# Weight preparation shared out anew over 64 expert steps, and the first weight chunks and token products moved

## The chip, the cores and the metric

The kernel runs on one NeuronCore of a Trainium2 chip. The metric is device time in microseconds (us), lower is better; several executions are timed and their median counts. One execution is also recorded by the hardware profiler, and its rows are what is read here.

The core has five engines with a queue of instructions each: TensorE (PE) multiplies matrices, VectorE (DVE), ScalarE (ACT) and GpSimd (POOL) compute element by element, SyncE (SP) issues most DMA transfers. They meet through semaphores; on its own queue each engine works strictly in order.

## The reference

Three blocks in a chain, cut to what matters:

```python
# 1. gated linear attention, B=4, H=8, S=768, D=48
f = 1 / (1 + exp(-f_logit))
state = f[t] * state + outer(k[t], v[t]);  y[t] = q[t] @ state
x = y as 3072 tokens x 384
# 2. mixture of 8 experts, the best one for each token
e = argmax(normalized(x) @ normalized(expert_emb).T / tau)
x = gate[:, None] * (relu(x @ w1[e]) @ w2[e])       # 384 -> 1024 -> 384
# 3. gated block
out = ((x @ w_a) * (x @ w_b)) @ w_out               # 384 -> 1536 -> 384
```

Inputs and outputs are float32 (w_a, w_b and w_out come as 64-bit floats of two words, which the kernel turns into 32 bits itself). Matrix products are made of a high and a low part of each operand, three products for each exact one.

## The kernel before

**Stages.** The attention scan lies from 0 to about 145 us, the experts from about 147 to 372 us, the gated block from there to the end at 805 us. The change touches the experts' stage and the first visits of the gated block.

**Expert steps.** The loop over s = 0 to 63 handles expert e = s // 8 and, with j = s % 8, one eighth of its hidden layer. A step issues, in this order: `h_part(s)`, nine matmuls into the PSUM tile `ph` (L1213 to L1215), ACT's high part `hh` (L1236) and DVE's low part `hl` (L1237) of its result; for j = 3 to 5 `x_turn`, a turn of the next expert's token rows, which gives DVE a subtraction (L1207); then `prep_run`, the weight preparation; then `w_more`, the splitting of the next experts' weights; and last `y_part(s - 1)`, nine matmuls into `po` (L1256), of which the last three read `hl` of the step before. The tile sizes tell the expert: 448 columns is expert 1 (steps 8 to 15), 432 expert 2, 416 expert 3, down to 384 for expert 7 (steps 56 to 63). After an expert's last product its outputs are copied to `yT` (L1272 on DVE).

So what `prep_run` and `w_more` give DVE in step s stands on DVE's queue behind `hl` of step s and ahead of `hl` of step s + 1.

**Weight preparation.** `prep_run(s, us)` gets a budget of planned microseconds: 1.4 in the first expert's steps, 2.1 in all others. It first runs what is due (deferred splits and stores), then takes pieces from two generators, `combines` first and `conv` with what remains, until the budget is used up; each piece states a planned cost. A piece that begins with budget left is finished, so a step can go over.

- `conv` turns weights to 32 bits, 18 blocks of 128x1536 words: ACT's absolute value, then DVE's L950 and L951 (planned 1.15), then L954 (0.95), then L957 for w_out or L988 for w_a and w_b (0.95). The blocks of w_out are split one slot later into high part (ACT) and low part (POOL, L964) and stored to DRAM. Three of the w_out blocks come first, those of w_a and w_b behind them; of the last three some pieces run in the gated block's slots.
- `combines` forms 15 weight matrices each of w_a (`combine(0)`) and of w_b (`combine(1)`) by sums on DVE (L1000, L1001, planned 0.7 each). A step later each is split by ACT and by POOL, in a few cases by DVE (L1036), and a step after that SP stores it to the DRAM tensor `wst` (L1056). Only when `combine(1)` is through, and s is over 60, are chunks 0 to 2 loaded by `w_chunk`.

**Splitting expert weights.** `w_more` runs `job_run`: every other step ACT makes the high part of a 128x1536 block, POOL subtracts two thirds of it and DVE one third (L895), so POOL is busy with a pair of subtractions in odd steps.

**Gated block.** A chunk of `wst` has eight matrices of 128x256 for each 128 partitions; `w_chunk(h)` loads one into a ring of three places (8 rows for even h, 7 for odd). They lie in the tile that held the last experts' weights, so a load waits for those products. `visit` multiplies six token products with six weight products (L1468 into `pv` and `pw`); every eight slots form a round of k1, k4, c1, k2, k5, c2, k3, k6, of which k4, k5 and k6 belong to the round before and are not made in round 0. Results go to `acc` by ACT (L1471 to L1475) and DVE (L1478, L1484). `prep_run` goes on every third slot with a budget of 1.0, and `x_prep` makes the token products: sums (L1348), ACT's high part (L1365) and the low part (L1356, DVE). The first group of them, `x_first`, is made on DVE during the last eight steps and the first three slots. `gate_ops` are the gate's small operations on DVE and ACT. Later on output products (L1497 to L1501 into `pq`) run between the visits.

**What sets the order.** It is written out by hand: instructions go to each engine's queue in the order in which the Python code issues them, and the budgets decide in which step a piece is issued. Before the change the lines in question are (the calls):

Of the kernel before, what the change touches and what calls it, by code (L numbers as in the profile page):

```python
# [6 lines left out]
F32 = mybir.dt.float32  # L7
# [21 lines left out]
NTT = NT // XT  # L29
# [18 lines left out]
NU = 8  # L48
# [8 lines left out]
def build(tc, I, out, dbg=None):  # L57
# [92 lines left out]
    with tc.manual_schedule():  # L150
# [920 lines left out]
                yield None  # L1071

        def w_chunk(h):
            if h < 2 * (NTT * NU + 1):
                n = 8 if h % 2 == 0 else 7
                SP.dma_start(out=WR[h % 3][:, 0:n].bitcast(F32), in_=wst[h % (2 * NU), :, 0:n])

        def combines():
            while phase[0] < 1:
                yield None  # L1080
            yield from combine(0)
            phase[0] = max(phase[0], 2)
            free[3] = free[4] = now[0]
            while phase[0] < 3:
                yield None
            free[3] = free[4] = free[5] = 1e9
            yield from combine(1)
            free[4] = now[0]
            phase[0] = 4
            while now[0] <= NE * FJ - 4:  # L1090
                yield None
            for h in range(3):
                w_chunk(h)

        streams = [combines(), conv()]

# [224 lines left out]
        def x_more():  # L1321
            for t in [t for t in acts if t not in X[NE - 1]] + list(X[NE - 1]):
                XS.extend(flat(t)[:, i * 512:(i + 1) * 512] for i in range(3))
# [48 lines left out]
        for s in range(NE * FJ):  # L1372
            e, j = divmod(s, FJ)
            h_part(s)
            if s == 0:
                ids_copy(0)
                rows_load_n(2)
                ids_store(0)
            if j == 0:
                y_part(s - 1)  # L1380
            if 3 <= j <= 5:
                x_turn(e + 1, j - 3)
            prep_run(s, 1.4 if s < FJ else 2.1)
            w_more(s)
            if 1 <= s <= 3:
                next(count_ops)
            n = 4 if e == 0 else 3
            if 0 <= j - 3 < n and e + 1 < NE:
                row_sq(e + 1, CAPS[e + 1] // 4, *[i for i in range(4) if min(i, n - 1) == j - 3])
            if j == n + 2:  # L1390
                ids_copy(e + 1)
            if j == n + 3 and e + 1 < NE:
                ids_store(e + 1)
                if e > 0:
                    rows_load_n(e + 2)
            if j > 0:
                y_part(s - 1)
            if s == IDS:
                SP.dma_start(out=idf, in_=heads[0:NT].rearrange("(t p) w -> p t w", p=128))
            if s == IDS + 4:  # L1400
                pf = ps_t.tile([128, 4, HP], F32, tag="t", name="pt")[:, 0, 0:1]
                T.matmul(out=pf, lhsT=ones[0:1], rhs=flag_b, start=True, stop=True)
                V.tensor_copy(fl_sb, pf)
                V.scalar_tensor_tensor(out=idx, in0=fl_sb.to_broadcast([128, NT // 128]), scalar=float(NT), in1=idf[:, :, 0],
                                       op0=ALU.mult, op1=ALU.add)
            if s == IDS:
                x_more()
            if s == IDS - 1:
                next(x_first)
            if s >= IDS:  # L1410
                for _ in range((2, 2, 1, 1, 1, 1, 3)[s - IDS]):
                    next(x_first, None)
            if s == IDS + 5:
                next(gate_ops)
# [127 lines left out]
        for at in range(8 * (NTT * NU + 1)):  # L1542
            P, rho = divmod(at, 8)
            if rho % 4 == 0 and at:
                w_chunk(at // 4 + 2)
            if at < 3:
                for _ in range(2):
                    next(x_first, None)
            name, late = SLOTS[rho]
# [247 lines left out]
```

## Time and profile before

| | |
|---|---|
| median of 3 runs | 808.38 us (807.41 to 810.64) |
| the profiled execution, its own time | 807.06 us |
| its span, first to last instruction | 805.2 us |
| mean granted TensorE clock | 0.990 |
| TensorE busy | 765.9 us (95%) |
| VectorE busy | 604.2 us (75%) |
| ScalarE busy | 419.8 us (52%) |
| GpSimd busy | 413.5 us (51%) |

Times in rows count from the span's start. A bracket at the end of a timeline row is the time for which the engine stood idle before it, and whose instruction ended that. Matmuls are pipelined, so rows of TensorE overlap. The granted clock is a share of full speed: 1.00 is 2.4 GHz, 0.50 is 1.2 GHz.

### The profile page before, as it was taken

To read this page: it belongs to the slowest core of one execution; us is meant where nothing else is said; L and a number is where in the kernel's file an instruction comes from. 1 tells how busy PE (TensorE), PEld (TensorE's weight loads), DVE (VectorE), ACT (ScalarE), POOL (GpSimd) and SP (SyncE) were. 2 spreads that over 40 slices of the span, in tenths; PEclk is the share of its full clock that TensorE was granted. 3 is DMA by queue.
4 is the path that set the end of the run, shared out by engine and by line. 5 is a ranking of instruction groups with operands and counts; after the bars stand their busy time and mean duration, and the time that the engine had idled before them with its cause. 6 is when DMAs were issued, how large, how long until landed. Compare 5 with 4: busy or idle time off the path is not lost.

```text
span 805.2 us, 16800 instructions
## 1 busy us (share of the span) xinstructions
PE 765.9 (95%) x6354; PEld 736.4 (91%) x6354; DVE 604.2 (75%) x1007; ACT 419.8 (52%) x889; POOL 413.5 (51%) x392
## 2 busy tenths in 40 slices
PE   7899989999999989988899999999999999999995
PEld 5899988989999989977798999999999999999995
DVE  7999995699978877696989567756766765686552
ACT  5899973666565746653444334434434434444331
POOL 6667773363468936972354154445326525343314
PEclk9999999999999999999999999999999999999998
DMA  7989752888499985978997998889888888988982
GB/s 278 327 301 325 238 189 88 277 275 266 154 294 265 325 270 150 289 215 290 345 414 266 352 323 302 301 299 339 309 297 328 312 294 320 330 297 295 335 305 88
DMA packets 83087, 226.82 MB, mean 282 GB/s; under 512 B 10649, under 2 KB 42247, under 8 KB 76727
## 3 DMA queue, kind: packets, MB, share of 16 engines
q1 hardware_dynamic: 79639, 216.10, 79.1%
q0 software_dynamic: 3072, 9.56, 3.1%
q8 instruction: 52, 0.85, 0.4%
q14 instruction: 36, 0.29, 0.1%
q10 hardware_dynamic: 288, 0.02, 0.0%
HBM read 192.95 MB, written 32.70 MB: 280 GB/s over the span
## 4 chain that ended last, share of the span: by engine, by line
PE 60%; DVE 19%; DMA 8%; issue 5%; ACT 4%; POOL 2%; SPq 0%; DVEq 0%; POOLq 0%; ACTq 0%
PE pv L1468 19%; PE po L1256 7%; PE pw L1468 5%; PE pq L1501 4%; PE pq L1499 4%; PE pq L1497 4%; DMA w<-wst 4%; PE ph L1213 3%; PE ph L1215 3%; PE ph L1214 3%; DVE a L1356 2%; DVE Rt L241 2%; DVE big L1445 2%; DVE big L1484 2%; DMA qkf<-qkf 2%
## 5 line engine op out<-in xcount | busy, mean ns | idle before, releaser
L1450 POOL TENSOR_TENSOR w<-big,w 128x512 fp32r<-128x512 f32 x72 | 94.7, 1330 | 172.6 <-ACT w L1449 169.8
L1468 PE MATMUL pv<-w,w 128*128 128x256 f32 x912 | 135.5, 283 | 9.1 <-DMA w<-wst 4.4
L1484 DVE TENSOR_TENSOR big<-big,pv 128x512 f32<-128x512 f32 x144 | 98.3, 682 | 58.3 <-PE pv L1468 58.3
L1468 PEld LDWEIGHTS pv<-w,w 128*128 128x128 f32 x912 | 126.3, 189 | 13.6 <-DVE big L1484 4.0
L1468 PE MATMUL pv<-a,w 128*128 128x256 f32 x816 | 120.3, 281 | 0.3
L1468 PEld LDWEIGHTS pv<-a,w 128*128 128x128 f32 x816 | 113.5, 188 | 2.1 <-DVE big L1478 1.1
L895 POOL TENSOR_TENSOR w<-raw,w 128x512 fp32r<-128x512 f32 x48 | 79.2, 1671 | 44.4 <-ACT w L892 41.1
L1501 PE MATMUL pq<-raw,w 128*128 128x384 f32 x288 | 97.2, 338 | 1.0 <-POOL w L1450 1.0
L1497 PE MATMUL pq<-raw,w 128*128 128x384 f32 x288 | 97.3, 338 | 0.0
L1499 PE MATMUL pq<-raw,w 128*128 128x384 f32 x288 | 96.9, 337 | 0.0
L1256 PE MATMUL po<-hh,w 128*128 128x224 f32 (+7 forms) x384 | 80.4, 344 | 0.0
L1478 DVE TENSOR_TENSOR big<-big,pv 128x256 f32<-128x256 f32 x96 | 40.3, 420 | 49.7 <-PE pv L1468 47.9
L1256 PEld LDWEIGHTS po<-hh,w 128*128 128x128 f32 x384 | 66.8, 190 | 1.3 <-DVE yT L1272 0.2
L1213 PE MATMUL ph<-a,w 128*128 128x224 f32 (+7 forms) x192 | 66.4, 346 | 0.0
L1215 PE MATMUL ph<-a,w 128*128 128x224 f32 (+7 forms) x192 | 66.3, 345 | 0.0
L1214 PE MATMUL ph<-a,w 128*128 128x224 f32 (+7 forms) x192 | 66.2, 345 | 0.0
L1445 DVE TENSOR_TENSOR big<-big 128x512 f32<-128x512 f32 x72 | 64.9, 929 | 1.7
L1449 ACT ACTIVATE w<-big 128x512 fp32r<-128x512 f32 x72 | 44.8, 633 | 37.0 <-DVE big L1445 37.0
L1236 ACT ACTIVATE hh<-ph 128x224 fp32r<-128x224 f32 (+7 forms) x64 | 31.4, 490 | 60.0 <-PE ph L1215 57.2
L1475 ACT ACTIVATE big<-pw 128x256 f32<-128x256 f32 x48 | 18.3, 382 | 78.1 <-PE pw L1468 78.1
L1501 PEld LDWEIGHTS pq<-raw,w 128*128 128x128 f32 x288 | 54.3, 189 | 1.6 <-POOL w L1450 1.6
L1256 PE MATMUL po<-hl,w 128*128 128x224 f32 (+7 forms) x192 | 45.6, 346 | 9.7 <-DVE hl L1237 9.6
(275 smaller groups left out, 1745.8 us busy)
## 6 DMA issues: line engine op xcount, KB each, us to landing
w<-wst SPq DMA_DIRECT2D x49, 1024.0 KB
w<-wst SPq DMA_DIRECT2D x49, 896.0 KB
raw<-wost SPq DMA_DIRECT2D x72, 384.0 KB
raw<-moe_w SPq DMA_DIRECT2D x32, 768.0 KB
qkf<-qkf SPq DMA_DIRECT2D x20, 768.0 KB
wst<-big SPq DMA_DIRECT2D x21, 512.0 KB
vx<-vx SPq DMA_DIRECT2D x24, 192.0 KB
big<-moe_w_out SPq DMA_DIRECT2D x6, 768.0 KB
```

The lines of the kernel that those rows point to most:

```text
L895: (G if i < NPOOL else V).tensor_tensor(out=wt[:, 1, f], in0=raw[:, f], in1=wt[:, 0, f].bitcast(F32), op=ALU.subtract)
L1213: T.matmul(out=out, lhsT=wh, rhs=xh, start=first, stop=False)
L1214: T.matmul(out=out, lhsT=wl, rhs=xh, start=False, stop=False)
L1215: T.matmul(out=out, lhsT=wh, rhs=xl, start=False, stop=last)
L1256: T.matmul(out=OS[e][k], lhsT=w[:, j % 4, k * 128:(k + 1) * 128], rhs=x, start=(j == 0 and w is wh and x is hh), stop=(j == FJ - 1 and x i ...
L1445: V.tensor_tensor(out=a, in0=a, in1=b, op=ALU.mult)
L1450: G.tensor_tensor(out=g[:, 1], in0=a, in1=g[:, 0].bitcast(F32), op=ALU.subtract)
L1468: T.matmul(out=out, lhsT=wt, rhs=xt_, start=first and j == 0, stop=j == 2, skip_group_check=True)
L1484: V.tensor_tensor(out=o, in0=o, in1=bank, op=ALU.subtract)
L1497: T.matmul(out=q, lhsT=gh, rhs=wh, start=(f == 0), stop=False)
L1499: T.matmul(out=q, lhsT=gh, rhs=wl, start=False, stop=False)
L1501: T.matmul(out=q, lhsT=gl, rhs=wh, start=False, stop=(f == F2J - 1))
```

## The change

Three things are changed.

- The budget of `prep_run` from step 8 on becomes 1.7 in steps with j = 3 to 5, those with a turn of rows, and 2.6 in the others, in place of 2.1 in all. Over eight steps that is 18.1 planned microseconds in place of 16.8.
- Chunk 0 is loaded at the end of step 60, chunk 1 at the end of step 62, both without the rows that round 0 does not read; only chunk 2 still waits for `combine(1)`.
- Of the token products, none is made in steps 61 and 62; the two moved pieces follow behind slot 3, which had none.

```diff
--- before.py
+++ after.py
@@ -1071,7 +1071,10 @@
                 yield None
 
         def w_chunk(h):
-            if h < 2 * (NTT * NU + 1):
+            if h < 2:
+                for lo, hi in ((0, 2), (4, 8)) if h == 0 else ((2, 5),):
+                    SP.dma_start(out=WR[h][:, lo:hi].bitcast(F32), in_=wst[h, :, lo:hi])
+            elif h < 2 * (NTT * NU + 1):
                 n = 8 if h % 2 == 0 else 7
                 SP.dma_start(out=WR[h % 3][:, 0:n].bitcast(F32), in_=wst[h % (2 * NU), :, 0:n])
 
@@ -1089,8 +1092,7 @@
             phase[0] = 4
             while now[0] <= NE * FJ - 4:
                 yield None
-            for h in range(3):
-                w_chunk(h)
+            w_chunk(2)
 
         streams = [combines(), conv()]
 
@@ -1380,7 +1382,7 @@
                 y_part(s - 1)
             if 3 <= j <= 5:
                 x_turn(e + 1, j - 3)
-            prep_run(s, 1.4 if s < FJ else 2.1)
+            prep_run(s, 1.4 if s < FJ else 1.7 if 3 <= j <= 5 else 2.6)
             w_more(s)
             if 1 <= s <= 3:
                 next(count_ops)
@@ -1405,10 +1407,12 @@
                                        op0=ALU.mult, op1=ALU.add)
             if s == IDS:
                 x_more()
+            if s in (NE * FJ - 4, NE * FJ - 2):
+                w_chunk((s + 4 - NE * FJ) // 2)
             if s == IDS - 1:
                 next(x_first)
             if s >= IDS:
-                for _ in range((2, 2, 1, 1, 1, 1, 3)[s - IDS]):
+                for _ in range((2, 2, 1, 1, 0, 0, 3)[s - IDS]):
                     next(x_first, None)
             if s == IDS + 5:
                 next(gate_ops)
@@ -1543,7 +1547,7 @@
             P, rho = divmod(at, 8)
             if rho % 4 == 0 and at:
                 w_chunk(at // 4 + 2)
-            if at < 3:
+            if at < 4:
                 for _ in range(2):
                     next(x_first, None)
             name, late = SLOTS[rho]
```

After the change all lines below the first piece of the diff have moved: L1207, L1237, L1272 and L1440 of before are L1209, L1239, L1274 and L1444.

**Place 1, DVE in steps 16 and 17.** Ahead of the first `hl` shown, that of step 17, there stand the pieces of step 16; between the first and the second `hl` those of step 17. L950 to L988 are one block of `conv`, L895 is DVE's third of a weight split. Before:

```order
L950 TENSOR_SCALAR ct<-ct 128x768
L951 TENSOR_SCALAR ct<-ct 128x768
L1237 SCALAR_TENSOR_TENSOR hl<-ph,hh 128x432
L954 SCALAR_TENSOR_TENSOR big<-big,ct 128x768
L988 SCALAR_TENSOR_TENSOR yT_2532<-big 128x256
L988 SCALAR_TENSOR_TENSOR yT_2533<-big 128x256
L988 SCALAR_TENSOR_TENSOR yT_2534<-big 128x256
L895 TENSOR_TENSOR w_2524<-raw,w_2524 128x512
L1237 SCALAR_TENSOR_TENSOR hl<-ph,hh 128x432
```

After:

```order
L950 TENSOR_SCALAR ct<-ct 128x768
L951 TENSOR_SCALAR ct<-ct 128x768
L954 SCALAR_TENSOR_TENSOR big<-big,ct 128x768
L988 SCALAR_TENSOR_TENSOR yT_2532<-big 128x256
L988 SCALAR_TENSOR_TENSOR yT_2533<-big 128x256
L988 SCALAR_TENSOR_TENSOR yT_2534<-big 128x256
L1239 SCALAR_TENSOR_TENSOR hl<-ph,hh 128x432
L895 TENSOR_TENSOR w_2524<-raw,w_2524 128x512
L1239 SCALAR_TENSOR_TENSOR hl<-ph,hh 128x432
```

L954 and three L988 have moved from behind `hl` of step 17 to ahead of it.

In the same way L957 of step 9, alone, has moved from behind `hl` of step 9 to ahead of it.

**Place 2, DVE in steps 24 to 26.** The three `hl` are those of steps 25, 26 and 27; L1000 is a sum of `combine(0)`, L1036 a low part of such a sum. Before:

```order
L1237 SCALAR_TENSOR_TENSOR hl<-ph,hh 128x416
L950 TENSOR_SCALAR ct<-ct 128x768
L951 TENSOR_SCALAR ct<-ct 128x768
L1036 TENSOR_TENSOR big<-yT_2533,big 128x4x128
L895 TENSOR_TENSOR w_66<-raw,w_66 128x512
L1237 SCALAR_TENSOR_TENSOR hl<-ph,hh 128x416
L1000 TENSOR_TENSOR yT_2534<-yT_2534,yT_2532 128x512
L1000 TENSOR_TENSOR yT_2533<-yT_2532,yT_2534 128x512
L954 SCALAR_TENSOR_TENSOR big<-big,ct 128x768
L1237 SCALAR_TENSOR_TENSOR hl<-ph,hh 128x416
```

After:

```order
L950 TENSOR_SCALAR ct<-ct 128x768
L951 TENSOR_SCALAR ct<-ct 128x768
L954 SCALAR_TENSOR_TENSOR big<-big,ct 128x768
L1036 TENSOR_TENSOR big<-yT_2533,big 128x4x128
L1239 SCALAR_TENSOR_TENSOR hl<-ph,hh 128x416
L1000 TENSOR_TENSOR yT_2534<-yT_2534,yT_2532 128x512
L1000 TENSOR_TENSOR yT_2533<-yT_2532,yT_2534 128x512
L988 SCALAR_TENSOR_TENSOR big<-big 128x3x256
L895 TENSOR_TENSOR w_66<-raw,w_66 128x512
L1239 SCALAR_TENSOR_TENSOR hl<-ph,hh 128x416 x2
```

L954 has moved ahead of `hl` of step 25, and the two L1000 ahead of `hl` of step 26, with an L988 that came later before; nothing is left between the last two `hl`.

**Place 3, SP at the end of the expert steps.** L1056 stores a product of `combine(1)`, L1076 (L1079 is the other branch after the change) loads a chunk, L1440 and L925 load a w_out block and a part of w_out. Before:

```order
L1056 DMA wst<-big 128x3x256
L1056 DMA wst<-big 128x256
L1056 DMA wst<-big 128x3x256
L1056 DMA wst<-big 128x256
L1056 DMA wst<-big 128x4x256
L1076 DMA w_2524<-wst 128x2048
L1076 DMA w_2524<-wst 128x1792
L1076 DMA w_2524<-wst 128x2048
L1440 DMA raw<-wost 128x768 x2
L925 DMA big<-moe_w_out 128x2x768
```

After:

```order
L1056 DMA wst<-big 128x3x256
L1056 DMA wst<-big 128x256
L1056 DMA wst<-big 128x3x256
L1056 DMA wst<-big 128x256
L1076 DMA w_2524<-wst 128x512
L1076 DMA w_2524<-wst 128x1024
L1056 DMA wst<-big 128x4x256
L1079 DMA w_2524<-wst 128x2048
L1076 DMA w_2524<-wst 128x768
L925 DMA big<-moe_w_out 128x2x768
L1444 DMA raw<-wost 128x768 x2
```

Chunk 0, now of two pieces, stands ahead of the last store; chunk 2 stands ahead of chunk 1.

Elsewhere on DVE, ACT and POOL the new budgets move pieces by one or two steps in the same manner. Steps 34 and 35 hold what steps 35 and 36 held (the two L1000 and L950, L951), steps 29 to 31 hold more than before, `combine(1)` comes to its end in step 59 in place of 60, and the three last blocks of `conv` in the gated block come three slots earlier. The POOL splits that follow from a sum or a block move with it.

## Rows read from the trace of the kernel before

**Rows 1.** The waits of TensorE, windows 225:290, 300:440, 120:806; us in total, times, longest

```profile
PE po L1256 <- DVE hl L1237: 4.0, 2, 3.2
...
PE po L1256 <- DVE hl L1237: 3.9, 3, 2.4
...
PE po L1256 <- DVE hl L1237: 9.6, 7, 3.2
```

**Rows 2.** The timeline of TensorE: start, us, engine, line, operation, tiles, [idle before]

```profile
173.80 0.88 PE L1256 MATMUL po<-hl,w 128*128 128x448 f32 x3 [0.72 <-DVE hl L1237]
...
283.89 0.82 PE L1256 MATMUL po<-hl,w 128*128 128x408 f32 x3 [3.17 <-DVE hl L1237]
...
362.94 1.18 PE L1256 MATMUL po<-hl,w 128*128 128x384 f32 x3 [2.40 <-DVE hl L1237]
```

**Rows 3.** Stretches: length, busy PE, PEld, DVE, ACT, POOL; clock, DMA, GB/s

```profile
285.00:290.00 5.00, 5.00 (x22) 4.96 (x21) 1.18 (x3) 1.21 (x3) 0.00 (x0) 0.70 1.02 325
...
360.00:365.00 5.00, 2.60 (x11) 1.83 (x10) 4.97 (x9) 1.09 (x4) 1.80 (x2) 0.81 0.35 105
365.00:370.00 5.00, 5.00 (x26) 5.00 (x25) 3.29 (x8) 1.03 (x3) 5.00 (x2) 0.85 0.64 136
370.00:375.00 5.00, 2.41 (x16) 2.12 (x15) 3.24 (x9) 2.24 (x6) 0.45 (x1) 1.00 0.96 328
```

**Rows 4.** The timelines of DVE and of POOL near 356 us

```profile
355.96 3.02 DVE L1000 TENSOR_TENSOR big<-big 128x512 f32<-128x512 f32 x2
...
356.74 3.40 POOL L895 TENSOR_TENSOR w<-raw,w 128x512 fp32r<-128x512 f32 x2
```

**Rows 5.** Lines L1000 and L988 by shape, 145:375 us; ns min/median/max, starts

```profile
L1000 DVE TENSOR_TENSOR big<-big x10: 676/1332/1672, 322.5 to 363.5; 128x512 f32<-128x512 f32 x10
...
L988 DVE SCALAR_TENSOR_TENSOR yT<-big x18: 408/417/1521, 183.9 to 219.8; 128x256 int32<-128x256 int32 x18
```

**Rows 6.** The timeline of DVE, steps 9 and 10

```profile
173.13 0.61 DVE L1237 SCALAR_TENSOR_TENSOR hl<-ph,hh 128x448 fp32r<-128x448 f32 x1
173.67 1.49 DVE L957 SCALAR_TENSOR_TENSOR big<-big 128x768 int32<-128x768 int32 x1
```

**Rows 7.** The timelines of DVE and of TensorE, step 17

```profile
200.78 0.60 DVE L1237 SCALAR_TENSOR_TENSOR hl<-ph,hh 128x432 fp32r<-128x432 f32 x1
201.30 0.95 DVE L954 SCALAR_TENSOR_TENSOR big<-big,ct 128x768 int32<-128x768 int32 x1
202.29 3.18 DVE L988 SCALAR_TENSOR_TENSOR yT<-big 128x256 int32<-128x256 int32 x3
...
204.09 0.75 PE L1256 MATMUL po<-hl,w 128*128 128x432 f32 x3
```

**Rows 8.** The timelines of DVE and of TensorE, steps 25 and 26

```profile
229.45 0.59 DVE L1237 SCALAR_TENSOR_TENSOR hl<-ph,hh 128x416 fp32r<-128x416 f32 x1 [1.90 <-ACT hh L1236]
...
234.14 0.58 DVE L1237 SCALAR_TENSOR_TENSOR hl<-ph,hh 128x416 fp32r<-128x416 f32 x1
...
236.97 0.73 PE L1256 MATMUL po<-hl,w 128*128 128x416 f32 x3
```

**Rows 9.** The timelines of TensorE and of DVE at the first visits

```profile
374.36 0.95 PE L1468 MATMUL pv<-w,w 128*128 128x256 f32 x6 [2.59 <-DMA w<-wst]
...
385.40 0.59 PE L1468 MATMUL pv<-w,w 128*128 128x256 f32 x3 [1.61 <-DMA w<-wst]
...
391.56 1.36 PE L1468 MATMUL pv<-w,w 128*128 128x256 f32 x9 [1.27 <-ACT big L1471]
...
377.22 1.32 DVE L1356 TENSOR_TENSOR a<-rows,a 128x256 fp32r<-128x256 f32 x3
...
384.69 0.55 DVE L950 TENSOR_SCALAR ct<-ct 128x768 f32<-128x768 f32 x1
```

**Rows 10.** The timelines of POOL and of TensorE at 433 us

```profile
433.23 2.32 POOL L964 TENSOR_TENSOR big<-big 128x768 fp32r<-128x768 f32 x1
...
436.49 0.63 PE L1468 MATMUL pv<-w,w 128*128 128x256 f32 x3 [0.92 <-DVE big L1484]
```

## The prediction

> **What bounds the kernel now.** I read the views in this order: the waits of TensorE (PE), its timeline, the timelines of VectorE (DVE) and GpSimd (POOL), the granted clock. PE is the bound: it is busy for 765.9 of 805.2 us, so time can only be won or lost where it stands still. In the 64 expert steps it stands still for one thing, the split `hl` (L1237) that DVE owes it: 9.6 us in all, of which 4.0 between 225 and 290 us and 3.9 from 300 us on [rows 1]. The single stalls are in front of the product of step 9 (0.72), step 38 (3.17) and step 60 (2.40) [rows 2]. After that of step 60 the clock is granted at 0.81 and 0.85 over two stretches of 5 us, which is full speed with a spell at 1.2 GHz in it; after the 2.59 us stall at 372 us it stays at 1.00 [rows 3]. 0.19 + 0.15 of 5 us is 1.7 us lost. Behind the 3.17 us stall the clock is 0.70 in one such stretch [rows 3], 1.5 us lost. Behind the steps come the hand-over's stalls: two for weight chunks (2.59, 1.61) and one for an evacuation on ScalarE (1.27) [rows 9].
>
> Why DVE is late is read from two rows side by side: from 355.96 us two L1000 sums take 3.02 us, while POOL needs 3.40 us for two subtractions begun at 356.74 [rows 4]. Alone an L1000 takes 0.68 us, at worst 1.67, and an L988 0.41 or 1.52 [rows 5]. So a DVE operation between SBUF tiles that meets POOL takes about an operation of POOL longer. The `hl` splits, which read PSUM, don't show this: 0.61, 0.60, 0.58 us [rows 6 to 8]. It follows that the weight preparation delays an `hl` by more than its own length where POOL is at work, which is each odd step (two subtractions of `job_run`) and, while products are split, once more in every step.
>
> The rule that speaks against the change is in the Trainium skill, "SBUF — State Buffer", "SBUF: two separate sides": VectorE and GpSimd share a port pair as an exclusive lock, and the loser blocks fully. The 3.02 us above agrees with it. By a shared bandwidth instead, the first two terms below would stay near their lower ends, and the forecast near the third rival.
>
> **The change part by part.** All terms are made against the profiled execution, 807.06 us (span 805.2); it lies 1.32 us under the median of 808.38, which I add at the end. A plus is time won.
>
> 1. Step 9. L957 now stands ahead of `hl` of step 9. That `hl` began at 173.13; L957 alone costs about what L954, as large, costs alone, 0.95 [rows 7], and if it ends where it ended before, at 173.67 + 1.49 = 175.16, it costs 2.03 [rows 6]. PE already waits for this `hl`, nothing hides it: −1.5, bounds −0.95 and −2.0.
>
> 2. Step 17. L954 and three L988 of step 17 move ahead of its `hl`: 0.95 + 3.18 = 4.13 us as they ran, 0.95 + 3 × 0.41 = 2.2 alone. That `hl` ended at 200.78 + 0.60 and was used at 204.09: slack 2.71 [rows 7]. So the stall is 1.4 as they ran. But steps 14 and 15 already carry three pieces more ahead of it, and the pair of step 17 on POOL then lies in the middle of these: one further POOL operation of some 1.5 us (half of the 3.40) at most. I take −2.3, bounds 0 and −2.9.
>
> 3. Steps 24 to 26. Ahead of `hl` of step 26 there now stand, beyond what stood there, an L954 (0.95), two L1000 (3.02 as in [rows 4], 1.36 alone), an L988 of L954's size (0.95) and a POOL split (some 1.5): 6.4 us, or 3.3 without any meeting. Against it: 234.14 + 0.58 to 236.97 is 2.25 of slack, and 1.90 in which DVE waited before step 25 [rows 8]. −2.3, bounds 0 and −3.0.
>
> 4. Steps 29 to 38. The two L1000 and L950 and L951 of step 36, and L954 of step 37, go to steps 34 and 35, L988 to step 36; the 3.17 us in front of step 38 go with them. But steps 33 to 35 now hold an L1001, four L1000, L950, L951, L954 and two L895 with five or six POOL operations, as many as steps 35 to 37 held; and steps 29 to 31 fill up as well. What is late next is `hl` of step 36. Of the 4.0 us [rows 1] I leave 3.0: +1.0, bounds +4.0 and −2.2 (the steps 29 to 31 lose as much again as step 26).
>
> 5. Steps 55 to 60. The preparation ends with step 59, not 60, so steps 55 to 59 hold seven such sums where five stood, and the same POOL work. What step 55 had idle takes part of it. 2 × 0.68 = 1.4 alone, 3.0 as run [rows 4]. Stalls of 3.9 [rows 1] become some 5.9: −2.0, bounds 0 and −3.5.
>
> 6. The clock. Each long stall may bring another spell at 1.2 GHz of up to 1.7 us [rows 3]; two were there, and the new stalls of steps 9, 17, 26 and 60 are of the length of the one at 2.59 that brought none. Half a spell more: −0.8, bounds +1.7 and −3.4.
>
> 7. The hand-over. Chunks 0 and 1 go out in steps 60 and 62 without their unused rows (0.75 and 0.375 MB instead of 1 and 0.875), chunk 2 behind the last store, which is a step earlier. SP has no wait in front that PE feels: the stores ahead wait for POOL and chunk 0 for the products of step 59. So 2.59 goes, and chunk 3, no longer behind two megabytes, should save its 1.61; and the gate's exponent no longer holds ScalarE up, 1.27 [rows 9]. Won: 5.5. Lost: between DVE's copy of the last output and the k2 evacuation there stand six token-product operations where three took 1.32 [rows 9], −1.2. And the w_out conversion moves three slots up: L950 and L951 (0.55 each) behind ScalarE's absolute value stand ahead of the k4 evacuation, L954 and L957 (0.95 each) ahead of that of k5, and the next visits to these banks wait for them: about −2.0, since no output products fill PE there yet. Net +2.3, bounds +1 and +4.
>
> 8. At 433 us. The last conversion's POOL split (2.32 us) precedes a PE wait of 0.92 [rows 10]; it moves three slots up, where POOL is free: +0.9, bounds 0 and +1.9 (a wait like it 3 us on).
>
> Taking the step turns, the PE work itself, all matmuls and the DMA bytes but 0.75 MB are unchanged and cost nothing.
>
> The sum: −1.5 − 2.3 − 2.3 + 1.0 − 2.0 − 0.8 + 2.3 + 0.9 = −4.7, so 807.06 + 4.7 = 811.8, and with the 1.32 **813.1 us**, 0.58% slower. (A measurement of this kernel tells about 0.5%, 4 us, from no change.)
>
> **The rivals.**
>
> Forecast, slower, 813.1 us: new stalls where steps without a turn of rows became heavier (9, 17, 26) and a longer one before step 60 eat what the hand-over gives. Chance 0.42; by its terms alone 812.5 to 821.
>
> First rival, faster: DVE's idle stretches take the moved pieces. For it: before step 25 DVE itself waits 1.90 us [rows 8], and every stall of steps 33 to 38 sits in a step with a turn of rows, which the change lightens. Against it: the pieces come in blocks of 2.6 us of planned work that POOL makes longer. It takes term 1 at −0.95, terms 2, 3 and 5 at 0, term 4 at +3, term 6 at +1, terms 7 and 8 as above: +6.3, so 800.8 + 1.32 = 802.1 us. It decides at the bound where the new blocks meet less than one POOL operation each. Chance 0.25.
>
> Second rival, no difference: stalls only change places. Terms 2 and 3 at −1.2 each, the rest as forecast: −2.5, 810.9 us. For it: the DVE and POOL work of the 64 steps is the same, and what one step gets another loses. Chance 0.33.
>
> Third rival, inside the other two: the hand-over does not give what it should because chunk 1 queues behind chunk 2, which waits for the last store to land. Then 2.59 comes back as a wait at c2, the fourth visit. Against it: the store is free a step earlier, about 3 us, and c2 comes some 4 us after the first visit. It costs up to 2.6 and would give 815.7 us with the other terms; its chance, 0.1, lies within the forecast's.
>
> **How the numbers follow.** Range 800 to 821: it holds the forecast and the second rival, and of the first what lies above 800; left out are a full success (all upper bounds, near 798) and stalls at their worst in steps 29 to 60 (near 824), about 0.1 each. The chances of faster, same and slower are those of the rivals: 0.25, 0.33, 0.42.
>
> **What would show it right or wrong.** In the trace of the changed kernel: a PE wait for `hl` of 2 to 3 us in front of step 9, one near step 17, one near step 26; none in front of step 38 but one near step 36; 5 to 7 us of them in steps 57 to 60; in all 15 us or so where there were 9.6. No wait of the first visit for its chunk; a wait for the k5 evacuation in the second round of visits. If the waits for `hl` from step 8 on sum to less than 9 us, the forecast's terms 2, 3 and 5 are wrong and the time is that of the first rival.

## The result: slower, by 0.6 to 1.0%

The changed kernel took 818.38 us in the median of four executions (816.83 to 818.59), the kernel before 808.18: a ratio of 1.0101, with a 95% interval of 1.0078 to 1.0124. Later the same kernel ran once more beside experiments: 813.84 us in five executions (811.97 to 816.46) against 809.43, ratio 1.0058, interval 1.0030 to 1.0085. Forecast were 813.1 us and slower. Why the means of the two sets lie 4.0 us apart is taken up below; the granted clock explains a part of it.

The profiled execution took 818.59 us (span 816.5, mean granted clock 0.984). First its waits of TensorE from 120 us on, to be set against [rows 1]; columns as there.

```profile
PE po L1258 <- DVE hl L1239: 13.0, 9, 3.2
PE pv L1472 <- DVE big L1488: 3.1, 5, 1.5
PE pw L1472 <- ACT big L1477: 2.5, 2, 1.3
PE po L1258 <- DVE yT L1274: 2.2, 2, 2.0
PE pq L1505 <- POOL w L1454: 1.6, 2, 0.8
...
PE pv L1472 <- DMA w<-wst: 0.9, 1, 0.9
PE pv L1472 <- DVE big L1482: 0.9, 2, 0.5
```

[Rows 1] show of the kernel before the waits for `hl` alone. Its waits in the gated block, in the same view:

```profile
PE pv L1468 <- DMA w<-wst: 4.4, 3, 2.6
PE pv L1468 <- DVE big L1484: 1.6, 3, 0.9
PE pv L1468 <- DVE big L1478: 1.3, 2, 1.0
PE pv L1468 <- ACT big L1471: 1.3, 1, 1.3
...
PE pq L1501 <- POOL w L1450: 1.0, 2, 0.8
PE pw L1468 <- ACT big L1473: 0.3, 1, 0.3
```

Then the single waits, from its timeline of TensorE: the products 9, 17, 25, 32, 44 and 60 of the expert steps, and four first visits of the gated block. They answer to [rows 2] and [rows 9].

```profile
175.10 1.39 PE L1258 MATMUL po<-hl,w 128*128 128x448 f32 x3 [2.83 <-DVE hl L1239]
...
208.74 0.86 PE L1258 MATMUL po<-hl,w 128*128 128x432 f32 x3 [1.20 <-DVE hl L1239]
...
239.17 0.83 PE L1258 MATMUL po<-hl,w 128*128 128x416 f32 x3 [1.08 <-DVE hl L1239]
...
265.95 1.01 PE L1258 MATMUL po<-hh,w 128*128 128x408 f32 x4 [2.02 <-DVE yT L1274]
...
312.88 0.81 PE L1258 MATMUL po<-hl,w 128*128 128x400 f32 x3 [1.83 <-DVE hl L1239]
...
370.79 1.33 PE L1258 MATMUL po<-hl,w 128*128 128x384 f32 x3 [3.17 <-DVE hl L1239]
...
385.76 0.62 PE L1472 MATMUL pw<-w,w 128*128 128x256 f32 x3 [1.33 <-ACT big L1477]
...
392.82 0.62 PE L1472 MATMUL pv<-w,w 128*128 128x256 f32 x3 [0.75 <-DVE big L1488]
...
396.72 1.34 PE L1472 MATMUL pv<-a,w 128*128 128x256 f32 x6 [1.48 <-DVE big L1488]
...
422.07 0.62 PE L1472 MATMUL pw<-w,w 128*128 128x256 f32 x3 [1.19 <-ACT big L1477]
```

Last the granted clock, in stretches of 5 us with columns as in [rows 3]: length, busy time of five engines, clock, share of the DMA engines, GB/s.

```profile
175.00:180.00 5.00, 4.90 (x19) 4.39 (x20) 1.21 (x4) 1.57 (x4) 3.10 (x2) 0.66 0.91 256
265.00:270.00 5.00, 4.05 (x15) 3.99 (x16) 2.67 (x5) 2.41 (x4) 4.01 (x3) 0.74 1.03 262
...
370.00:375.00 5.00, 4.21 (x13) 3.76 (x14) 1.89 (x6) 0.00 (x0) 3.96 (x1) 0.50 0.55 161
...
385.00:390.00 5.00, 3.90 (x19) 3.69 (x20) 2.31 (x6) 1.50 (x4) 0.00 (x0) 0.69 0.58 203
395.00:400.00 5.00, 3.52 (x20) 3.31 (x19) 4.23 (x8) 1.66 (x4) 1.86 (x1) 0.71 0.26 56
```

The clock's cost is estimated as (1 - clock) times 5 us over all 54 stretches from 145 to 415 us: 3.4 us before, 10.2 us after. That is its full price, as if TensorE had lost time in the whole of each spell. With it the two profiled executions balance, in us:

| where TensorE lost time | before | after | change |
|---|---|---|---|
| waits for `hl` | 9.6 | 13.0 | +3.4 |
| waits for the output copy `yT` | 0 | 2.2 | +2.2 |
| waits of the visits, for DMA, DVE and ACT | 8.9 | 7.4 | -1.5 |
| waits of output products for POOL | 1.0 | 1.6 | +0.6 |
| the clock at 1.2 GHz, 145 to 415 us | 3.4 | 10.2 | +6.8 |

The sum is +11.5 us, and 818.59 - 807.06 is 11.5 (the spans lie 11.3 apart). That it closes to a tenth is partly luck, since the clock row is an estimate: the products 9 to 15, behind which the clock was lost in the changed kernel alone, came 1.5 us farther apart for a spell priced at 1.7.

### The profile page after: what moved, and what is told of

It reads as the page before. It is cut to its first block, busy times and chain, and to the rows that moved or that the text cites. A ratio compares the mean times of both kernels' runs of the same rounds, so it can differ in the third digit from the quotient of the medians.

```text
span 816.5 us, 16797 instructions
## 1 busy us (share of the span) xinstructions
PE 772.8 (95%) x6354; PEld 741.3 (91%) x6354; DVE 604.2 (74%) x1007; ACT 420.0 (51%) x889; POOL 408.3 (50%) x392
## 4 chain that ended last, share of the span: by engine, by line
PE 55%; DVE 26%; DMA 5%; issue 5%; ACT 4%; POOL 3%; DVEq 0%; SPq 0%; POOLq 0%; ACTq 0%
PE pv L1472 20%; PE pw L1472 5%; PE pq L1505 5%; PE pq L1503 5%; PE pq L1501 5%; PE po L1258 4%; DMA raw<-moe_w 3%; DVE Rt L241 2%; DVE big L1488 2%; DVE Bt L230 2%; DVE big L1449 2%; DVE a L1358 2%; PE ph L1215 2%; PE ph L1217 2%; PE ph L1216 2%
## 5 line engine op out<-in xcount | busy, mean ns | idle before, releaser
L1472 PE MATMUL pv<-w,w 128*128 128x256 f32 x912 | 138.0, 287 | 3.7 <-DVE big L1488 1.6
L1472 PEld LDWEIGHTS pv<-w,w 128*128 128x128 f32 x912 | 128.9, 193 | 8.0 <-DVE big L1488 3.9
L895 POOL TENSOR_TENSOR w<-raw,w 128x512 fp32r<-128x512 f32 x48 | 76.8, 1619 | 49.9 <-ACT w L892 48.3
```

Of the source, the lines that this page charges most:

```text
L895: (G if i < NPOOL else V).tensor_tensor(out=wt[:, 1, f], in0=raw[:, f], in1=wt[:, 0, f].bitcast(F32), op=ALU.subtract)
L1472: T.matmul(out=out, lhsT=wt, rhs=xt_, start=first and j == 0, stop=j == 2, skip_group_check=True)
```

## The experiments

**One part at a time.** The budgets alone:

```diff
-            prep_run(s, 1.4 if s < FJ else 2.1)
+            prep_run(s, 1.4 if s < FJ else 1.7 if 3 <= j <= 5 else 2.6)
```

> The new budgets alone (1.7 in steps with a turn of rows, 2.6 in the others); chunks and token products as before. Theory: the budgets carry the loss, by longer waits for hl in the steps made heavier (9, 17, 32, 44, 60), by spells of the clock at 1.2 GHz behind the longest of them, and by the last conversions in the gated block, which come three slots earlier because combine(1) ends a step earlier. It expects 815 to 819 us, and about 9 us more than before by the product of step 61. Rival: the moved chunks and token products carry the 5 us that were lost behind step 63. It expects 812 to 814 us here.

Measured: 814.33 us (812.45 to 815.61, six executions) against 807.85; ratio 1.0066, interval 1.0042 to 1.0091. That lies between the two expectations, 0.7 us under the theory's range and 0.3 us over the rival's. The ratio decides: the budgets alone cost as much as the changed kernel's second set shows. Product 61 came 7.0 us later than before (9 was expected), with the same waits at the products 9, 17, 25 and 44 as in the changed kernel (2.81, 1.24, 1.08, 1.82 us). From product 62 to the end of the span, 811.9 - 378.1 = 433.8 us passed, before 805.2 - 371.1 = 434.1. So the last conversions, which the theory had named too, cost nothing on the whole there: waits of 0.72, 1.48, 1.15 and 1.19 us came among the visits, but no visit waited for a chunk. With the budgets alone the wait of 2.59 us for chunk 0 [rows 9] is gone already. And the clock was lost in 365 to 375 us alone, 3.4 us of it, as much as before.

The early, shorter chunk loads alone:

```diff
         def w_chunk(h):
+            if h < 2:
+                for lo, hi in ((0, 2), (4, 8)) if h == 0 else ((2, 5),):
...
-            for h in range(3):
-                w_chunk(h)
+            w_chunk(2)
...
+            if s in (NE * FJ - 4, NE * FJ - 2):
+                w_chunk((s + 4 - NE * FJ) // 2)
```

> The early, shorter loads of chunks 0 and 1 alone. Theory: the wait of 2.59 us for chunk 0 and most of the 1.61 us for chunk 3 go and nothing else moves: 804 to 806 us. Rival (the moved loads are what costs): 809 to 812 us, with new waits of the first visits for DVE or for a chunk.

Measured: 805.87 us, ratio 0.9978 (0.9963 to 0.9993), as the theory had it, some 2 us less; but by another way than it said. The wait for chunk 0 is gone, and chunk 3 has taken part of it, 2.98 us in place of 1.61 [rows 9]:

```profile
383.07 0.77 PE L1472 MATMUL pv<-w,w 128*128 128x256 f32 x3 [2.98 <-DMA w<-wst]
```

The move of the token products alone:

```diff
-                for _ in range((2, 2, 1, 1, 1, 1, 3)[s - IDS]):
+                for _ in range((2, 2, 1, 1, 0, 0, 3)[s - IDS]):
...
-            if at < 3:
+            if at < 4:
```

> The move of the token products alone, from steps 61 and 62 to behind slot 3. Theory: DVE has room in steps 61 and 62, so nothing is won there; six operations in place of three behind the last output cost at most 1.3 us in front of the first k2, part of it hidden by the wait for chunk 0: 808 to 809.5 us. Rival: the moved products carry the loss at the first visits: 811 to 813 us.

Measured: 808.44 us, ratio 1.0000 (0.9982 to 1.0019), as the theory had it. The price forecast for the first k2 is there, 1.21 us for the evacuation that stands on ScalarE behind the token products (0.29 before). First before, then here:

```profile
378.59 0.62 PE L1468 MATMUL pw<-w,w 128*128 128x256 f32 x3 [0.29 <-ACT big L1473]
```

```profile
379.90 0.62 PE L1468 MATMUL pw<-w,w 128*128 128x256 f32 x3 [1.21 <-ACT big L1473]
```

It costs nothing on the whole because chunk 3 has time to land meanwhile: its wait of 1.61 us is gone.

Both moves with the old budgets:

> Both moves with the old budgets. Theory: the sum of the two single runs against before, 804 to 807 us, faster than before. Rival (they lose behind step 63 whatever the budgets): 811 to 814 us.

Measured: 806.90 us, ratio 0.9987 (0.9970 to 1.0004): inside the theory's range, about 1 us less than before and not clear of no change. The rival falls. With the old budgets the moves don't cost what was lost behind product 63.

**Do the parts add up?** The changed kernel unaltered, beside the experiments that follow.

> The changed kernel once more, unaltered, beside the others of this group. Theory 1 (the parts add up; the changed kernel's 818 us had two to four more spells at 1.2 GHz than usual by chance): 812.5 to 816 us, as far from before as budgets alone and the two moves together give, +6.5 - 1.0. Theory 2 (the moves cost something only where the new budgets are in force): 817 to 819 us again.

Measured: 813.84 us, ratio 1.0058. The parts add up: +0.66% for the budgets and -0.13% for the moves make +0.53%. What set the first set apart is the clock in part. The mean granted clock of its four executions was 0.985, that of these five 0.990, and the means of the times, 818.04 and 814.07, lie 4.0 us apart. At full price, (0.9900 - 0.9852) x 816 us, the clock would make 3.9 us. But over the 71 executions of the kernel before beside the experiments, a clock lower by 0.0048 went with 1.8 us only, and the mean clock counts stretches where nothing is left to slow down (0.50 from 800 us to the end of the profile before, where TensorE does nothing). So about half is accounted for, and the rest stays open. The kernel before, in the second set, had 0.989.

**Is it POOL that makes DVE late?** In the changed kernel POOL's two thirds of an expert weight's low part are cut to 64 of 512 columns each; the rest of these low parts is left out.

```diff
-                f = slice(i * 512, (i + 1) * 512)
+                f = slice(i * 512, i * 512 + 64 if i < NPOOL else (i + 1) * 512)
```

> The changed kernel with POOL's share of the expert weights' low parts cut to 64 of each 512 columns (the rest of these low parts is left out, so POOL is busy for some 65 us less); DVE's queue is unchanged. Theory (a DVE operation that meets POOL takes longer by about an operation of POOL, and that is what makes the new blocks late): DVE's L1000 falls from 1.0 to 1.7 us to about 0.7 to 1.0 in the median, the waits of TensorE for hl fall from 13.0 to under 6 us, and the time to 806 to 811 us. Rival (the number of operations ahead of hl alone makes it late): hl waits of 10 us or more, 814 to 818 us.

Measured: 802.97 us, ratio 0.9928 (0.9904 to 0.9953), 11 us less than the changed kernel beside it and 3 us below what the theory expected. DVE's 1007 instructions are the same, and its busy time falls from 604.5 to 575.1 us; the median of the ten L1000 of w_a falls from 1.30 to 0.69 us, that of w_b stays at 0.69. Step 17 shows how, first in the changed kernel, then here: DVE's three L988 and POOL's two subtractions.

```profile
204.99 3.17 DVE L988 SCALAR_TENSOR_TENSOR yT<-big 128x256 int32<-128x256 int32 x3
...
204.40 3.15 POOL L895 TENSOR_TENSOR w<-raw,w 128x512 fp32r<-128x512 f32 x2 [3.78 <-ACT w L892]
```

```profile
203.70 1.35 DVE L988 SCALAR_TENSOR_TENSOR yT<-big 128x256 int32<-128x256 int32 x3
...
203.85 0.92 POOL L895 TENSOR_TENSOR w<-raw,w 128x64 fp32r<-128x64 f32 x2 [5.84 <-ACT w L892]
```

The three take 1.35 us in place of 3.17, `hl` is ready in time, and the wait of 1.20 us at product 17 is gone; so are those of the products 32 and 44, while one of 1.07 us at product 43 is longer than the 0.49 it was. The waits for `hl` sum to 6.0 us (13.0 in the profile of the changed kernel). The largest left, 2.59 us at product 9, is a control: there POOL runs the subtraction of another line, L887, which was not cut. So POOL's work is what makes DVE late in the changed kernel. But POOL stands beside DVE before the change too, and that kernel was not run with short subtractions: what the new budgets cost when POOL is out of the way isn't shown.

**Does an idle TensorE bring the spells at 1.2 GHz?** Products that nobody reads are put in front of the longest waits.

```diff
+        FILL = {9: (3, 13), 32: (1, 10), 44: (3, 9), 60: (3, 18)}
...
+                    if FILL.get(s, (9, 0))[0] == (k if x is hh and w is wh else 3 if x is hl and k == 0 else -1):
+                        fill = ps_t.tile([128, 4, HP], F32, tag="t", name="pt").rearrange("p a b -> p (a b)")[:, 0:n_of(e)]
+                        for _ in range(FILL[s][1]):
+                            T.matmul(out=fill, lhsT=wh[:, j % 4, 0:128], rhs=hh, start=True, stop=True)
```

> The changed kernel with products that nobody reads on TensorE in front of its four longest waits of the expert steps: 13 in front of hl of product 9, 10 in front of the second output tile of product 32, 9 in front of hl of product 44, 18 in front of hl of product 60, about as long as the waits were (2.83, 2.02, 1.83, 3.17 us). Theory (TensorE's idle time, not its late results, brings the spells at 1.2 GHz): the products behind come when they came, and no spell follows in the expert steps; against the changed kernel 2 to 5 us less, and the clock at 1.00 from 150 to 372 us. Rival (the spells come by chance or from something else): as many spells as before, and the time equal or up to 2 us longer where a filler outlasts its wait.

Measured: 814.82 us, ratio 1.0075 (1.0049 to 1.0101). The time missed the expectation; it lies in the rival's range, up to 2 us longer. One filler had a price of its own: that of product 44, a step with a turn of rows, waited 2.3 us for a buffer of the turn, and behind it lies the one spell left in the steps (0.75 from 310 to 315 us). So the other three once more, without it:

> The changed kernel with products that nobody reads at products 9, 32 and 60 only; the one at product 44, a step with a turn of rows, had to wait for a buffer of the turn and cost 2.3 us of its own. Theory (idle TensorE brings the spells at 1.2 GHz, and the filled waits are where most of them start): no spell between 150 and 380 us, the granted clock of the whole run higher by 0.002 to 0.004 than the changed kernel's on the same chip (0.990 in the mean of five executions), and 1.5 to 3.5 us less than its 813.8 us: 810 to 812.5 us. Rival (the spells come by chance): the clock as before and 813 to 816 us.

Measured: 815.83 us, ratio 1.0092 (1.0065 to 1.0119), mean clock 0.991 in six executions: the time missed again, by 3 us, and the clock rose by 0.001 rather than 0.002 to 0.004. By its time, and nearly by its clock, it is the rival that came. One spell was left in the steps, behind the wait of 1.83 us at product 44 (0.85 and 0.80 from 310 to 320 us). At the place itself it went as the theory says. Product 60, filled: the filler, the products behind it without a wait, and the clock of the stretch; then the same stretch of the changed kernel in the later run.

```profile
368.26 3.28 PE L1262 MATMUL pt<-hh,w 128*128 128x384 f32 x18
371.63 0.79 PE L1263 MATMUL po<-hl,w 128*128 128x384 f32 x3
...
370.00:375.00 5.00, 4.92 (x28) 4.33 (x28) 2.89 (x8) 0.49 (x1) 4.80 (x2) 1.00 0.63 199
```

```profile
370.00:375.00 5.00, 5.00 (x19) 5.00 (x19) 0.68 (x2) 0.49 (x1) 1.42 (x1) 0.58 0.52 176
```

The changed kernel's two profiles and that of the budgets alone lose the clock behind product 60 (0.50, 0.58 and 0.52 in this stretch), the two with a filler don't. But a wait does not bring a spell each time: behind product 9 the changed kernel lost the clock after 2.83 us of waiting, while with the budgets alone it was kept after 2.81. And what the fillers saved was spent elsewhere, since `hl` still came late at other products (1.10 us at product 41, which had no wait in the profiles of the changed kernel). Of the filled waits only that of product 44, whose filler had to wait itself, was followed by a spell. Still, that the spells follow idle time is supported at product 60 alone, where all three unfilled profiles with these budgets had one; what a filler is worth, and why the whole time did not fall, stays open.

**Is it the slack of `hl`?** The three products that read `hl` come one step later, behind the next `h_part`; for this a third buffer of `ph` takes the place of the fourth of `po`. With the early chunks, on the kernel before:

```diff
-            h_part(s)
+            h_mm(s, range(KC))
+            if s >= 2 and j != 1:
+                y_part(s - 2, (1,))
+            h_split(s)
...
             if j > 0:
-                y_part(s - 1)
+                y_part(s - 1, (0,))
```

Here `(0,)` stands for the six products with `hh`, `(1,)` for the three with `hl`; an expert's last `hl` products are not delayed. In the runs with the early chunks, chunk 0 goes out one step later than in the changed kernel, behind the late products of step 59.

> The kernel before with the early chunk loads and one more change: the three products of y_part that read hl come a step later, behind the next h_part, with a third PSUM buffer for ph in place of the fourth for po, so hl may come some 2.4 us later. Theory (TensorE is the bound and only late hl stops it in the steps): the waits for hl, 9.6 us, fall to 0 to 2 us and the spell behind product 38 goes: 793 to 798 us. Rival (DVE's work is the limit; the late splits show up elsewhere, as waits of h_part for a free ph or of y_part for the output copies): 803 to 807 us.

Measured: 802.01 us (798.88 to 803.62), ratio 0.9931 (0.9907 to 0.9956): the best version, faster than both kernels, though 4 us short of the theory. The profiled execution was the fastest of the five, 798.88 us at a clock of 0.998 (the others 0.988 to 0.993), so its waits show what is left even without a spell:

```profile
PE pv L1479 <- DMA w<-wst: 4.6, 2, 3.1
PE po L1261 <- DVE hl L1239: 3.0, 3, 1.4
PE po L1261 <- DVE yT L1277: 2.3, 1, 2.3
```

The waits for `hl` fell from 9.6 to 3.0 us and no spell came between 145 and 415 us in this execution, but a wait of 2.3 us for the output copy came up, and the visits still waited 4.6 us for chunks, where 4.4 stood before. Without the early chunks:

> The kernel before with the three hl products one step later and nothing else. Theory: of the 7.4 us that this and the early chunks won together, the chunks gave 2 and the later products 5 to 6, so 803 to 805 us, and the wait for chunk 0 comes back with 2 us or more. Rival (the two gain only together): 806 us or more.

Measured: 806.34 us, ratio 0.9978 (0.9958 to 0.9999); the theory, 803 to 805, was too hopeful, and the time lies in the rival's range, that the two gain only together. The wait for chunk 0 grew from 2.59 us to:

```profile
372.31 1.62 PE L1475 MATMUL pv<-w,w 128*128 128x256 f32 x6 [6.27 <-DMA w<-wst]
```

Each alone wins some 2 us; the two together win 7.4 by the medians and 5.6 by the ratio. The product of the two single ratios, 0.9956, is just the end of the interval of both, so that they win more together is likely, not certain. The trace shows why it should be so: time won in the steps is taken back by the chunk unless it is loaded earlier. And on the changed kernel:

> The changed kernel with the three hl products one step later (a third buffer for ph; chunk 0 one step later, behind the late products of step 59). Theory (the new budgets cost only because hl has so little slack): the blocks of 2.6 us fit, the waits for hl fall from 13 to 1 to 4 us, and the time comes to 799 to 804 us, within 3 us of the 802.0 us with the old budgets. Rival (the blocks are longer than any slack, DVE and POOL are the limit in steps 24 to 37): 805 to 809 us.

Measured: 806.84 us, ratio 0.9971 (0.9950 to 0.9992). The rival's range holds it. More slack wins some 7 us here too (1.0058 to 0.9971), but the new budgets still cost against the old ones (0.9971 to 0.9931, intervals that just touch), and the waits say the same:

```profile
PE po L1261 <- DVE hl L1239: 6.1, 7, 1.9
PE po L1261 <- DVE yT L1277: 3.0, 1, 3.0
```

So too little slack is a part of the story, about half by the ratios: with the moves in place the new budgets cost 0.0071 of the time with the small slack (0.9987 to 1.0058) and 0.0040 with the larger. In places the blocks of 2.6 us are longer than the larger slack as well.

**What does work on POOL cost DVE?** The best version, with the middle third of each low part on DVE:

```diff
-NPOOL = 2
+NPOOL = 1
```

> The kernel before with the early chunk loads and the hl products one step later, and with the middle third of each expert weight's low part on DVE in place of POOL. Theory (a DVE operation that meets POOL loses about as long as POOL's operation takes, so a third on POOL costs DVE as much as doing it): DVE's busy time in the expert steps changes by less than 6 us though it gets some 30 operations more of 0.68 us, L1000 falls to a median of 0.7 to 1.0 us, and the time lies at 799 to 804 us, 0.988 to 0.995 of before. Rival (meeting POOL costs DVE little, and DVE simply gets 16 to 20 us more): 806 to 812 us, and more waits for hl than 3.0 us.

Measured: 804.76 us, ratio 0.9958 (0.9942 to 0.9974), the time 1 us above the theory's range and below the rival's. The waits for `hl` were 2.1 us, not more than 3.0 as the rival had it, those for the output copy 4.0 in place of 2.3. The mechanism came out in its direction. The first part of both pages, busy time, share and instructions of each engine, with two thirds on POOL and with one:

```profile
PE 761.7 (96%) x6354; PEld 732.7 (92%) x6354; DVE 608.3 (76%) x1007; ACT 421.5 (53%) x889; POOL 409.2 (51%) x392
```

```profile
PE 766.3 (96%) x6354; PEld 736.5 (92%) x6354; DVE 612.9 (77%) x1035; ACT 420.9 (53%) x889; POOL 365.0 (46%) x364
```

DVE executed 28 operations more, which alone take 28 x 0.68 = 19 us, and was busy for 4.6 us more; the median of the ten L1000 of w_b fell from 1.22 to 0.77 us. So some 14 of the 19 us had been paid before, as DVE operations that POOL made longer. This is an estimate: DVE's busy time differs by up to 6 us (602.7 to 608.3) between kernels with the same 1007 DVE operations. It is also less than the theory's price. POOL was busy for 44.2 us less, 1.6 us for each of the 28 operations, and 14 us is a third of that: a DVE operation that met POOL paid a part of POOL's operation, not the whole. The Trainium skill ("Perfetto Trace Analysis", "Optimizing Scalar/DVE Operations") says that shifting work between VectorE and GpSimd may not help, as they share a port; these rows agree: the exchange won nothing.

## Why the prediction was right, step by step

Its direction held, its range held both sets, and its forecast of +0.58% is what the second set measured. Its terms held less well than their sum, and that the forecast agrees with the second set to the digit is luck: term 4 came out better and a loss that was not listed came in. Measured is how much farther apart the starts of `hl` products stand in the profile of the changed kernel than before; a plus is time won.

| term | forecast | products | measured |
|---|---|---|---|
| 1, step 9 | -1.5 | 8 to 9 | -2.1 |
| 2, step 17 | -2.3 | 15 to 18 | -1.9 |
| 3, steps 24 to 26 | -2.3 | 24 to 28 | -1.4 |
| 4, steps 29 to 38 | +1.0 | 29 to 40 | +2.2 |
| not forecast | 0 | 41 to 45 | -2.9 |
| 5, steps 55 to 60 | -2.0 | 55 to 60 | -1.0 |
| 6, the clock | -0.8 | 145 to 415 us | -6.8 |
| 7 and 8, the hand-over | +3.2 | 62 to the end, clock set aside | +1.1 |

Terms 1 to 5 sum to -7.1 us as forecast, and to -7.1 as measured with the row that was missing, which is luck again: the misses of the five, -0.6, +0.4, +0.9, +1.2 and +1.0, and the missing -2.9 cancel. (Product 8 came 0.8 us earlier, which is no term: nothing ahead of it is changed. With it all measured rows sum to -12.0, where the spans lie 11.3 apart; the clock stands at full price.)

The rule on which the terms rest, that a DVE operation that meets POOL takes about an operation of POOL longer, was set too high. The terms suffered little, as most were priced from the same pieces as they ran. The rule "about an operation of POOL longer" does not come out of [rows 4]: two sums that met two subtractions of 1.7 us took 1.7 us longer together, so half an operation each, and the run with one third on POOL gives about a third. (That a shared bandwidth would bring the forecast near the third rival is a slip too: with terms 1 and 2 at their smaller bounds it comes to 810.2 us, near the second. And the list of single stalls left out 0.96 us in the first expert's steps and 0.80 us at product 32.)

**Term 1** was mis-sized, a little beyond its bound: L957 ahead of `hl` met one subtraction of POOL (L887, 1.99 us from 171.70).

```profile
170.04 2.53 DVE L954 SCALAR_TENSOR_TENSOR big<-big,ct 128x768 int32<-128x768 int32 x1
172.61 1.90 DVE L957 SCALAR_TENSOR_TENSOR big<-big 128x768 int32<-128x768 int32 x1
174.43 0.61 DVE L1239 SCALAR_TENSOR_TENSOR hl<-ph,hh 128x448 fp32r<-128x448 f32 x1
```

1.90 us stand where 1.49 did [rows 6], and against product 8 the block ahead of it began 0.2 us later. **Terms 2 and 3** lie within their bounds; the stall forecast before product 26 stood before product 25. That POOL is what lengthens the operations in them was shown by the run with short subtractions.

**Term 4** had the right sign and the wrong follower. The stall of 3.17 us [rows 2] went, with its spell, and that at product 36 didn't come (profiles of other executions show 0.2 us there). What came was a wait that I had not listed: product 32 is the first of an expert and needs its output tile copied away, and that copy stood on DVE behind two L1000 moved ahead of it.

```profile
260.90 3.39 DVE L1000 TENSOR_TENSOR yT<-yT,yT 128x512 f32<-128x512 f32 x2
...
265.32 0.57 DVE L1274 COPY yT<-po 128x416 f32 x1
```

**The row not forecast** is the step that failed outright: I took steps 39 to 54 for unchanged. There the pieces of `conv` moved too, but ScalarE's absolute value had to wait for the block's load, and with it DVE.

```profile
302.49 0.90 ACT L948 ACTIVATE ct<-big 128x768 f32<-128x768 f32 x1 [3.25 <-DMA big<-moe_w_b]
...
303.42 0.56 DVE L950 TENSOR_SCALAR ct<-ct 128x768 f32<-128x768 f32 x1 [3.36 <-ACT ct L948]
...
309.86 1.88 DVE L954 SCALAR_TENSOR_TENSOR big<-big,ct 128x768 int32<-128x768 int32 x1
```

DVE stood idle for 3.36 us and then had the whole block and the next one's beginning ahead of `hl` of the products 43 and 44, in turn steps; at the second it also met POOL's pair. A larger budget can't do work whose data has not come, and the work then falls into the steps that were to be spared.

**Term 5** stayed below its size: the waits at the products 57, 58 and 60 came to 1.16 + 0.65 + 3.17 = 5.0 us, where 3.9 stood [rows 1] and 5.9 were forecast.

**Term 6** is the one that was most mis-sized in the first set: 6.8 us where 0.8 was forecast, twice its bound. With the budgets alone the profile lost no more clock than before, and the second set's mean clock was that of the kernel before, though its profiled execution lost 8.6 us. Over all nine executions of the changed kernel the mean clock was 0.988 (0.9879), over the 71 of the kernel before 0.989 (0.9887): 0.7 us at full price. So the term is an average near 0.8 with a spread of several microseconds from one execution to the next.

**Terms 7 and 8.** The gains came as listed (the first of them with the budgets alone too): no wait for chunk 0, chunk 3 (0.75 us for DVE stands there now) or the gate's exponent. The two losses came too, 1.33 us at the first k2, where 0.29 stood, and 0.75 + 1.48 us behind the w_out pieces, for 1.2 and 2.0 forecast. Missed were two more of the second round, 0.89 us for a chunk and the 1.19 us at 422.07. The latter is term 8 gone wrong: the split did leave its old place at 433 us, whose 0.92 us [rows 10] went, and POOL was free three slots up, idle for 7.25 us. But the split then stood on POOL's queue ahead of the token sums of the next group, on which ScalarE and then TensorE waited.

```profile
417.71 1.87 POOL L964 TENSOR_TENSOR big<-big 128x768 fp32r<-128x768 f32 x1 [7.25 <-ACT big L963]
419.54 0.73 POOL L1350 TENSOR_TENSOR rows<-yT,yT 128x256 f32<-128x256 f32 x1
```

Of the signs named in advance there came: the waits before the products 9 and 17, none before 38, 5.0 us at 57 to 60, 13.0 us in all for `hl` where about 15 were named (15.2 with the copies, which the sign did not name), no first visit waiting for its chunk, and the k5 wait (1.48 us). There did not come the one near 36, and 26 was 25. The third rival, chunk 1 behind chunk 2, showed nowhere.

## What to carry to other kernels

A budget of planned time spreads work evenly only if each piece takes as long everywhere: a piece that meets another engine's work can cost twice its own time (here 3.17 us beside GpSimd's long subtractions, 1.35 beside short ones), and a piece whose load has not landed moves on into the steps that should stay light. Before work is levelled over steps, ask what makes the deadline so near; here a third PSUM buffer for the hidden layer and early loads won 6 to 7 us together where each alone won 2. When a kernel's stalls are of the length after which the clock falls in some executions, one profile shows one draw: compare several executions' clocks before a difference of 0.5% is explained.

## What the runs showed of the hardware

VectorE operations between SBUF tiles take longer beside GpSimd's work: three of 128x256 took 3.17 us beside two subtractions of 128x512 and 1.35 beside two of 128x64. When 28 subtractions of 0.68 us, 19 us in all, went from POOL to DVE, POOL was busy for 44.2 us less and DVE for 4.6 us more, so by that estimate POOL's 44 us had cost DVE 14. The splits `hl` of the experts 1 to 7, which read PSUM, kept to 0.54 to 0.63 us in all profiles. The rule of the Trainium skill ("SBUF — State Buffer", "SBUF: two separate sides") that VectorE and GpSimd hold a common port pair as an exclusive lock agrees with both; no run here tells a lock from a shared bandwidth.

The same program can lose more or less to the 1.2 GHz level from one execution to the next: the nine executions of the changed kernel had mean clocks from 0.984 to 0.994. Between 145 and 415 us the profiles of this study lost from 0 (the best version) to 10.2 us (the changed kernel; 8.6 in its second profile), and waits of the same place and length (2.83 and 2.81 us) were followed by it in one and not in the other. What decides that, these runs don't show.
